# Weight conversion in an attention and softplus kernel: the low words rounded by ScalarE and added by GpSimd, with a new order of the work

## The chip, the core and the metric

The kernel runs on one core of a Trainium2 chip. The metric is the device time of one execution in microseconds; lower is better. The core has five engines with queues of their own: TensorE (PE, whose weight loads are shown apart as PEld), VectorE (DVE), ScalarE (ACT), GpSimd (POOL) and SyncE (SP), which here issues nearly all transfers.

## The reference

Linear attention without softmax, a norm by head, and then two matrix products with softplus between them, for 8 images of 576 rows with 8 heads of 64:

```python
kv  = np.einsum('bhsd,bhse->bhde', k, v)
out = np.einsum('bhsd,bhde->bhse', q, kv)
rms = np.sqrt(np.mean(out * out, axis=-1, keepdims=True) + 1e-06)
x   = (out / rms * g_norm).astype(np.float32)      # then (B,H,S,D) -> (4608, 512)
h = x @ w_in                                        # w_in: 512 x 2048
g = np.maximum(h, 0.0) + np.log1p(np.exp(-np.abs(h)))
return (g @ w_out).astype(np.float32)               # w_out: 2048 x 512
```

The two weight matrices arrive as 64-bit floating-point numbers; everything else is 32 bits wide.

## The kernel before, in words

**Products.** Every matrix product of the feed-forward part is made with operands cut into three pieces: a high one, the remainder, and a third that joins the two. ScalarE makes the high piece, VectorE the others. A product then takes three matrix multiplications.

**Stages.** The feed-forward part works on 16 chunks of 128 inner columns each (c = 0 to 15). In the first stage 12 blocks of 384 tokens go through the first 4 to 6 chunks (`step`: line 864 multiplies x by the first matrix, line 886 is softplus, lines 888, 875 and 879 cut the result into pieces, line 871 multiplies by the second matrix). In the second stage blocks of 512 tokens go through the other chunks, in pairs, by a scheme with fewer products (`wide_step`: lines 1066 and 1137). Partial sums of the first stage are written to memory and read again.

**Attention.** For each image `kv_of` loads keys and values and multiplies them (line 696), and `rows` turns the queries, multiplies (line 720), squares and sums (line 724), takes the root on GpSimd (lines 727 and 728), multiplies by it (line 732) and turns the result for the products (line 738). This is spread over the first 300 us. `split` cuts a tile of x into its pieces (lines 640, 643, 646).

**Weights.** Tile j is chunk c = j // 2 of the first matrix (j even) or of the second (j odd). `weight` fetches one tile of 128x512 doubles (512 KB, line 423) into a raw buffer, of which there is one ("raw") and, for the odd tiles of the first eight chunks, another one ("rawb"). Then it makes 32-bit numbers of it. The high word is moved into the form of a 32-bit number in two VectorE steps (lines 438 and 442). ScalarE squares the top 16 bits (line 434), so that VectorE's mask (line 447) can set numbers that are too small to zero; ScalarE also counts those beyond a limit (line 451). In the version before, three more VectorE steps add the rest of the mantissa: line 455 takes the power of two of the number, line 460 multiplies it by the low word, and line 464 adds the product to the number. After that `split_weight` cuts the result into three pieces (lines 501 to 529), or the tile is written back to memory for the second stage (line 482).

**Order.** The order of all instructions is fixed before the launch. Every piece of work is a task with an engine, an assumed duration, a position, tasks that it waits for and buffers that it takes and gives back. The planner (`Plan.order`) goes through them in assumed time: on each engine it takes, of the tasks that can begin, the one with the smallest position. Transfers can also be tied behind a step of the first product. Each queue then runs its instructions strictly in that order. The positions are computed from the lists P0 to P7: `CONVERT` and `FETCH` place the first eight weight tiles, `TAKEN` those of chunks 6 to 15, P4 the row tiles, P5 the images, P6 the loads of the second stage, P7 the first images' loads. Where the plan sees TensorE idle in the beginning, it puts in multiplications of the identity by itself (line 1232), whose result nobody reads.

The two VectorE steps that make the high word, in their order, and the three that follow the mask stand in the listing.

## Time and profile before

| What | Value |
|---|---|
| median of 3 runs | 858.48 us (857.46, 858.48, 860.58) |
| span of the profiled execution | 856.4 us; its own time is not given beside it |
| TensorE busy | 843.0 us (98%) |
| VectorE busy | 704.1 us (82%) |
| ScalarE busy | 520.6 us (61%) |
| GpSimd busy | 76.6 us (9%) |
| bytes moved | 167.07 MB |

The span runs from the first instruction of the profile to the last; the time of a run is a little longer. The profile gives busy time by engine, by stretch of the span, and by group of instructions (line, engine, operation, output and inputs with their shapes, count; busy us and mean ns of one; idle time of the engine before them and what ended it). A busy TensorE is partly modelled, so a difference of a few tenths of a microsecond in its records means nothing. The granted TensorE clock is 1.00 in all stretches.

### The profile page before, as it was taken

How to read it: one execution, taken by the hardware profiler on the slowest of the kernel's cores; microseconds unless marked ns; L12 is line 12 of the kernel's file. 1: busy time of each engine (PE TensorE's matmuls, PEld its weight loads, DVE VectorE, ACT ScalarE, POOL GpSimd, SP SyncE). 2: the span in 40 equal slices, each digit the busy share in tenths (PEclk: the TensorE clock that was granted, in tenths of full speed). 3: DMA queues.
4: the chain of work that ended last, by engine and by line, in shares of the span. 5: the costliest groups of instructions: out<-in, count | busy, mean ns of one | idle time of the engine just before them, and what ended most of it. 6: DMA issues, size and time to landing. Idle time of an engine off the chain costs nothing.

```text
span 856.4 us, 17075 instructions
## 1 busy us (share of the span) xinstructions
PE 843.0 (98%) x6464; PEld 754.1 (88%) x6464; DVE 704.1 (82%) x995; ACT 520.6 (61%) x980; POOL 76.6 (9%) x79
## 2 busy tenths in 40 slices
PE   8899999999999999999999999999999999999998
PEld 5578898999898999999999999998999899999996
DVE  7888898888788889798898788878788766788873
ACT  6766665446344567766667665655868555566654
POOL 0351223111113300000000000000000000000000
PEclk9999999999999999999999999999999999999999
DMA  9998997778884755436644546645364753777864
GB/s 283 297 233 212 261 273 232 185 245 218 214 188 119 194 160 185 142 110 207 210 156 154 180 151 206 195 158 181 124 197 138 234 168 102 240 237 246 249 189 131
DMA packets 239778, 167.07 MB, mean 195 GB/s; under 512 B 106320, under 2 KB 198736, under 8 KB 239696
## 3 DMA queue, kind: packets, MB, share of 16 engines
q1 hardware_dynamic: 239392, 165.86, 65.9%
q8 instruction: 50, 0.82, 0.4%
q14 instruction: 32, 0.26, 0.1%
q10 hardware_dynamic: 304, 0.13, 0.1%
HBM read 112.98 MB, written 52.95 MB: 194 GB/s over the span
## 4 chain that ended last, share of the span: by engine, by line
PE 94%; ACT 1%; DVE 1%; DMA 1%; issue 1%; POOL 0%; SPq 0%; POOLq 0%; DVEq 0%; ACTq 0%
PE banks L1137 31%; PE banks L1066 28%; PE banks L871 16%; PE banks L864 15%; PE banks L720 2%; PE banks L696 2%; DMA loads<-in_k_dram 1%; PE banks L738 0%; PE banks L1232 0%; PE banks L776 0%; DVE units L643 0%; DVE half L732 0%; DVE roots L724 0%; POOL roots L728 0%; ACT w L783 0%
## 5 line engine op out<-in xcount | busy, mean ns | idle before, releaser
L1137 PE MATMUL banks<-pieces,gv 128*128 128x512 f32 x768 | 236.8, 390 | 0.0
L1137 PE MATMUL banks<-pieces,g_False 128*128 128x512 f32 x384 | 149.4, 389 | 0.0
L1137 PEld LDWEIGHTS banks<-pieces,gv 128*128 128x128 f32 x768 | 132.5, 188 | 17.2 <-DVE banks L910 0.2
L864 PE MATMUL banks<-units,pieces 128*128 128x384 f32 x768 | 144.8, 337 | 0.0
L871 PE MATMUL banks<-pieces,gv 128*128 128x512 f32 x576 | 143.3, 393 | 0.0
L864 PEld LDWEIGHTS banks<-units,pieces 128*128 128x128 f32 x768 | 134.7, 188 | 4.5
L871 PEld LDWEIGHTS banks<-pieces,gv 128*128 128x128 f32 x576 | 106.2, 188 | 19.0
L1066 PEld LDWEIGHTS banks<-units,pieces 128*128 128x128 f32 x840 | 111.0, 188 | 6.5 <-ACT banks L1112 0.4
L1066 PE MATMUL banks<-units,pieces 128*128 128x256 f32 x840 | 115.2, 280 | 0.0
L886 ACT ACTIVATE half<-banks 128x384 f32<-128x384 f32 x64 | 31.4, 491 | 94.0 <-PE banks L864 90.7
L1127 DVE TENSOR_TENSOR gv<-g_True,gv 128x1024 fp32r<-128x1024 f32 x47 | 57.5, 1223 | 35.6 <-ACT gv L1124 35.5
L1137 PEld LDWEIGHTS banks<-pieces,g_False 128*128 128x128 f32 x384 | 72.1, 188 | 15.0
L1066 PEld LDWEIGHTS banks<-units,w 128*128 128x128 f32 x504 | 66.7, 188 | 3.7 <-ACT banks L1112 0.2
L1066 PE MATMUL banks<-units,w 128*128 128x256 f32 x504 | 69.6, 280 | 0.0
L728 POOL TENSOR_TENSOR roots<-roots,half 128x8 f32<-128x8 f32 x36 | 62.3, 1731 | 3.0
L1130 DVE SCALAR_TENSOR_TENSOR g_False<-gv 128x1024 fp32r<-128x1024 f32 x47 | 57.6, 1225 | 1.5
L1029 DVE TENSOR_TENSOR units<-loads,units 128x1024 fp32r<-128x1024 f32 x42 | 51.2, 1219 | 6.0 <-ACT units L1026 5.9
L1094 ACT ACTIVATE g_True<-banks 128x256 f32<-128x256 f32 x96 | 36.7, 384 | 30.6 <-PE banks L1066 29.9
L1116 DVE TENSOR_TENSOR g_True<-banks,g_True 128x512 f32<-128x512 f32 x48 | 33.1, 690 | 25.8 <-PE banks L1066 19.8
L931 ACT ACTIVATE m<-banks 128x512 f32<-128x512 f32 x72 | 42.1, 595 | 18.2 <-PE banks L1137 12.5
L1032 DVE SCALAR_TENSOR_TENSOR units<-units 128x1024 fp32r<-128x1024 f32 x42 | 51.4, 1224 | 1.7
L1026 ACT ACTIVATE units<-loads 128x1024 fp32r<-128x1024 f32 x42 | 44.3, 1056 | 12.4 <-PE banks L1066 10.1
(115 smaller groups left out, 1248.7 us busy)
## 6 DMA issues: line engine op xcount, KB each, us to landing
loads<-x SPq DMA_DIRECT2D x180, 128.0 KB, 2.7
part<-m SPq DMA_DIRECT2D x72, 256.0 KB, 3.1
m<-part SPq DMA_DIRECT2D x72, 256.0 KB, 3.4
loads<-form SPq DMA_DIRECT2D x45, 256.0 KB, 3.2
form<-loads SPq DMA_DIRECT2D x36, 256.0 KB, 3.0
raw<-in_moe_w_in_dram SPq DMA_DIRECT2D x16, 512.0 KB, 4.7
loads<-in_k_dram SPq DMA_DIRECT2D x32, 256.0 KB, 4.0
loads<-in_v_dram SPq DMA_DIRECT2D x32, 256.0 KB, 4.5
```

Of the source, the lines that this page charges most:

```text
L728: nc.gpsimd.tensor_tensor(out=r.tile, in0=r.tile, in1=half, op=ALU.pow)
L864: nc.tensor.matmul(from_the_end(hp, w), lhsT=w_in.tile[:, i, kd * P:(kd + 1) * P], rhs=from_the_end(xv.tile[:, i, kd], w), start=(m == 0), ...
L871: nc.tensor.matmul(mine[i].tile, lhsT=gv.tile[:, m, i * P:(i + 1) * P], rhs=w_out.tile[:, m], start=(c == cs[0] and m == 0), stop=(c == cs ...
L931: a = add("ACT", 690 if ph == LAST else 600, lambda: nc.scalar.activation(new(ot, [P, d_model]), bank.tile, func=AF.Copy, scale=scale if p ...
L1026: nc.scalar.activation(part_of(0, F32R), xl.tile if m > 1 else xl.tile[:, 0], func=AF.Copy, scale=DOWN)
L1029: nc.vector.tensor_tensor(out=part_of(1, F32R), in0=xl.tile if m > 1 else xl.tile[:, 0], in1=part_of(0), op=ALU.subtract)
L1032: nc.vector.scalar_tensor_tensor(out=part_of(2, F32R), in0=part_of(1), scalar=-RADIX, in1=part_of(0), op0=ALU.mult, op1=ALU.add)
L1066: nc.tensor.matmul(from_the_end(place(q), (16, 8)[kd]), lhsT=w[:, m, at:at + P], rhs=from_the_end(dst.tile[:, m, v, kd] if u < 6 else dst. ...
L1094: nc.scalar.activation(dst, src, func=AF.Softplus, scale=1.0 + E)
L1127: nc.vector.tensor_tensor(out=gvt(1, F32R), in0=gt(), in1=gvt(0), op=ALU.subtract)
L1130: nc.vector.scalar_tensor_tensor(out=gt(F32R), in0=gvt(1), scalar=-RADIX, in1=gvt(0), op0=ALU.mult, op1=ALU.add)
L1137: nc.tensor.matmul(from_the_end(mine[i].tile, P), lhsT=(gvt(m, F32R) if m < 2 else gt(F32R))[:, c, i * P:(i + 1) * P], rhs=from_the_end(ou ...
```

## The change

After the mask, the low word is no longer multiplied by the number's power of two and added as a floating-point number. ScalarE reads the low word as an integer, multiplies it by 2^-29 and writes it as a rounded 32-bit integer, which is the number of units in the last place that the low word stands for. GpSimd adds it to the bits of the masked number as integers. The result stays in the buffer of the masked number, so a tile takes two buffers of the ring "m" where it took three, and the raw buffer is given back after the two steps on the high word, the square and the rounding.

The three VectorE steps (lines 455, 460, 464) are gone; the rounding is a new ScalarE task without a wait on VectorE, and the add is a GpSimd task that waits for the mask and the rounding. All lists of positions have new values, and with them the order of every queue may differ.

The diff; of the lists of positions only P0 and P2 are shown:

```diff
--- before.py
+++ after.py
@@ -9,6 +9,7 @@
 F32 = mybir.dt.float32
 F32R = mybir.dt.float32r
 U32 = mybir.dt.uint32
+I32 = mybir.dt.int32
 BF16 = mybir.dt.bfloat16
 AF = mybir.ActivationFunctionType
 ALU = mybir.AluOpType
@@ -252,15 +253,15 @@
     STEPS = [(ph, n, p) for ph in (1, 2) for n in range(n_wide) for p in PAIRS[ph - 1][n]]
     LAST = 2
 
-    P0 = [-45.94, -26.77, -11.8, 0.28, -29.91, -5.64, -2.86, 3.84, -103.4, -98.98, -69.3, -76.66, -68.5, -24.67, -23.22, -34.97, 8.15, -43.02, 7.47, 9.69, 7.18, 18.16, -12.1, 4.75, 1.0, 106.19, 31.3, 6.28, 7.19, 5.22]
...
+    P0 = [-8.08, -21.9, 1.52, -3.72, -1.69, -21.85, -3.44, 4.58, -19.16, -116.42, -126.81, -30.71, -114.11, 66.57, 59.07, -8.96, 11.38, -40.88, 20.33, 9.06, 7.18, 13.51, -12.61, 4.48, 3.76, 2.72, -67.19, 5.29, 10.05, 8.61]
...
     CONVERT, FETCH, EARLY, LATER = P0[:8], P0[8:16], P0[16:27], P0[27:]
...
-    P2 = [24.08, 35.56, 23.68, 37.26, 50.08, 83.13, 74.26, 112.0, 102.25, 108.09, 139.38, -110.13, 88.34, 208.35, 423.47, -209.77, 170.15, -245.78, 423.49, 179.94, -7.53]
...
+    P2 = [28.72, 32.86, 29.3, 39.52, 59.02, 78.06, 93.3, 120.52, 78.04, 106.2, 67.37, 66.51, 64.28, 60.53, 65.65, 67.32, 70.96, 65.85, 87.14, 65.55, -8.62]
...
     SPLIT = {p: (P1[i], P1[6 + i]) for i, p in enumerate((2, 3, 4, 5, 6, 7))}
     TAKEN = {c: (P2[c - 6], P2[4 + c]) for c in range(6, 16)}
     LEAD, APART, AHEAD, MM2, LATE, SPLIT_G = P3[0], P3[1], P3[2], P3[3:11], P3[11:14], P3[14]
@@ -425,7 +426,7 @@
 
         f = add("SP", 450, fetch, (), fetch_pos, [raw], size=1800, behind=behind)
         if wide:
-            sq, t, p = (slot(n) for n in ("sq", "m", "m"))
+            sq, t, r = slot("sq"), w, slot("m")
 
             def words_of():
                 return raw.tile[:, :, 0], raw.tile[:, :, 1]
@@ -451,27 +452,21 @@
                 nc.scalar.activation(sq.tile, sq.tile, func=AF.Identity, scale=2.0 ** -126, bias=big,
                                      accum_out=over[:, j:j + 1])
 
-            def power():
-                nc.vector.tensor_scalar(out=new(p, [P, d_model], U32), in0=t.tile, scalar1=0xFF800000,
-                                        scalar2=None, op0=ALU.bitwise_and)
-
-            def rest():
-                pf = p.tile.bitcast(F32)
-                nc.vector.scalar_tensor_tensor(out=pf, in0=words_of()[0], scalar=2.0 ** -52, in1=pf,
-                                               op0=ALU.mult, op1=ALU.mult)
+            def rounded():
+                nc.scalar.activation(new(r, [P, d_model], I32), words_of()[0], func=AF.Copy, scale=2.0 ** -29)
 
             def total():
-                nc.vector.tensor_tensor(out=new(w, [P, d_model]), in0=t.tile.bitcast(F32),
-                                        in1=p.tile.bitcast(F32), op=ALU.add)
+                nc.gpsimd.tensor_tensor(out=t.tile.bitcast(I32), in0=t.tile.bitcast(I32),
+                                        in1=r.tile, op=ALU.add)
+                t.tile = t.tile.bitcast(F32)
 
             a1 = add("ACT", 670, square, [f], pos, [sq], [raw])
+            a2 = add("ACT", 670, rounded, [f], pos, [r], [raw])
             d1 = add("DVE", 430, high1, [f], pos, [t], [raw])
             d2 = add("DVE", 690, high2, [d1], pos, [], [raw])
             d3 = add("DVE", 690, mask, [d2, a1], pos, [])
             over_done.append(add("ACT", 910, beyond, [d3], pos + (4 if c < 4 else 0), [], [sq]))
-            d4 = add("DVE", 430, power, [d3], pos, [p, w])
-            d5 = add("DVE", 690, rest, [d4], pos, [], [raw])
-            ready = add("DVE", 690, total, [d3, d5], pos, [], [t, p])
+            ready = add("POOL", 1200, total, [d3, a2], pos, [], [r])
         else:
             ready = add("DVE", 450, lambda: nc.vector.tensor_copy(new(w, [P, d_model]), raw.tile[:, :, 0]),
                         [f], pos, [w], [raw])
```

12 lines of the change are left out of this document (6 added, 6 removed).

## The prediction

> **What bounds the kernel now.** I read the profile page first, then TensorE's filler matmuls by stretches, then all engines by stretches, then the groups of the weight conversion, then single instructions of GpSimd and VectorE in order of time. The head of the page:
>
> ```profile
> span 856.4 us, 17075 instructions
> PE 843.0 (98%) x6464; PEld 754.1 (88%) x6464; DVE 704.1 (82%) x995; ACT 520.6 (61%) x980; POOL 76.6 (9%) x79
> PE   8899999999999999999999999999999999999998
> ```
>
> TensorE is busy for 98% of the span, so all that can be won lies in its other 13.4 us and in busy time that is not useful. Useless busy time exists: line 1232 multiplies the identity by itself where the plan saw TensorE idle. Its windows (columns: stretch, length, TensorE busy with these instructions, weight loads, granted clock, DMA share, GB/s):
>
> ```profile
> 0.00:20.00 20.00, 10.99 (x29) 6.92 (x29) 1.00 0.96 286
> 20.00:40.00 20.00, 5.21 (x15) 2.43 (x15) 1.00 1.05 298
> 40.00:60.00 20.00, 2.14 (x7) 1.24 (x7) 1.00 0.94 228
> 60.00:80.00 20.00, 0.50 (x1) 0.19 (x1) 1.00 0.85 214
> 80.00:856.00 776.00, 0.00 (x0) 0.00 (x0) 1.00 0.64 189
> ```
>
> All engines in other stretches (busy us: TensorE, its loads, VectorE, ScalarE, GpSimd; then clock, DMA share, GB/s):
>
> ```profile
> 0.00:4.70 4.70, 3.09 (x7) 2.49 (x8) 1.59 (x7) 1.28 (x1) 0.69 (x6) 1.00 0.54 168
> 4.70:60.00 55.30, 47.40 (x651) 35.74 (x649) 49.15 (x82) 41.72 (x82) 16.94 (x17) 1.00 1.02 280
> 60.00:80.00 20.00, 19.89 (x253) 16.45 (x252) 17.45 (x32) 11.76 (x24) 6.28 (x6) 1.00 0.85 214
> 80.00:140.00 60.00, 60.00 (x585) 53.71 (x585) 54.16 (x93) 37.09 (x73) 15.61 (x14) 1.00 0.90 244
> 140.00:300.00 160.00, 160.00 (x1528) 144.09 (x1528) 135.70 (x235) 76.25 (x151) 37.03 (x36) 1.00 0.76 203
> 300.00:560.00 260.00, 260.00 (x1600) 236.94 (x1599) 223.77 (x298) 172.14 (x327) 0.00 (x0) 1.00 0.54 172
> 560.00:856.00 296.00, 292.63 (x1852) 264.63 (x1850) 222.29 (x253) 180.40 (x324) 0.00 (x0) 1.00 0.59 185
> ```
>
> The reader is to see two kernels in one. From 80 us to the last matmul TensorE never stops and has no fillers: nothing in there can be shortened by relieving VectorE, it can only be lengthened. Before that lies the ramp. Between 4.7 and 60 us TensorE idles 55.30 - 47.40 = 7.9 us, and fillers take 10.99 + 5.21 + 2.14 less the 3.09 before 4.7, that is 15.25 us. These 23.2 us are the ceiling of any gain. In the ramp VectorE is busy 49.15 of 55.30 us (89%) and the DMA share is 1.02. Either of them may set it. VectorE's part in it shows in the order of its work: the first real step of the feed-forward part begins at 44 us, the seventh weight is converted only at 54 us, and the eighth is begun at 60 us:
>
> ```profile
> 44.09 2.07 PE L864 MATMUL banks<-units,pieces 128*128 128x384 f32 x11
> 54.39 0.68 DVE L464 TENSOR_TENSOR m<-m,m 128x512 f32<-128x512 f32 x1
> 60.02 0.42 DVE L438 TENSOR_SCALAR m<-g 128x512 uint32<-128x512 uint32 x1
> ```
>
> **The change, removed.** Of each of the 32 weight tiles three VectorE instructions go (columns of the groups: busy us, mean ns, idle before):
>
> ```profile
> L455 DVE TENSOR_SCALAR m<-m 128x512 uint32<-128x512 uint32 x32 | 13.6, 424 | 1.2 <-DMA part<-m 0.4
> L460 DVE SCALAR_TENSOR_TENSOR m<-raw,m 128x512 f32<-128x512 uint32 x24 | 16.5, 686 | 0.5
> L460 DVE SCALAR_TENSOR_TENSOR m<-g,m 128x512 f32<-128x512 uint32 x8 | 5.5, 692 | 0.2
> L464 DVE TENSOR_TENSOR m<-m,m 128x512 f32<-128x512 f32 x32 | 22.0, 687 | 0.7
> ```
>
> Together 13.6 + 16.5 + 5.5 + 22.0 = 57.6 us, 1.80 us for one weight. Seven weights are converted before 60 us: 7 x 1.80 = 12.6 us of VectorE leave the ramp. The other 25 leave stages in which TensorE is full: worth nothing.
>
> **Added on ScalarE.** One more pass over the raw words for each weight. Its nearest row reads the same buffer over as many elements:
>
> ```profile
> L434 ACT ACTIVATE sq<-raw 128x512 bf16<-128x512 bf16 x24 | 16.1, 673 | 2.7 <-DMA raw<-in_moe_w_in_dram 2.1 <-DMA raw<-in_moe_w_out_dram 0.5
> ```
>
> It costs 0.67 us, 32 x 0.67 = 21.5 us in all, 4.7 us in the ramp, where ScalarE is idle 55.30 - 41.72 = 13.6 us. I take it as hidden; bounds are 0 and 4.7 us, if ScalarE's order puts each one ahead of a copy that TensorE waits for. It can run while VectorE assembles the high word.
>
> **Added on GpSimd.** One integer add of 128x512 with two SBUF inputs for each weight. The trace has no such instruction. Its rows are these:
>
> ```profile
> L728 POOL TENSOR_TENSOR roots<-roots,half 128x8 f32<-128x8 f32 x36 | 62.3, 1731 | 3.0
> L727 POOL TENSOR_SCALAR roots<-roots 128x8 f32<-128x8 f32 x36 | 13.2, 366 | 205.2 <-DVE roots L724 204.1
> masks.py:199 POOL TENSOR_SCALAR_AFFINE_SELECT early<-early 128x128 f32<-128x128 f32 x1 | 0.3, 292 | 0.1
> ```
>
> Below, the add costs at least the 0.29 us of a quarter as many elements; above, the power's 1.73 us. I take four times the 128x128 row, 1.17 us, since that row is the nearest in kind: it streams elements. The Trainium skill, GPSIMD Engine Reference, § 3.1, gives 4497 ns for a two-input add of 2048 elements against VectorE's 2293 and advises against elementwise work there; scaled to 512 elements that is an estimate of about 1.1 us, so the sum would not move by it, and no run here shows it yet.
>
> The add waits for VectorE's mask and for ScalarE's rounding. Queued behind it on GpSimd is the root of the next row tile (lines 727 and 728, together about 2 us), for which VectorE's line 732 waits, and that sends the transposes to TensorE. So a root can come up to 1.17 us later, and an add up to 2 us later behind a root. GpSimd has the room: 16.94 us of 55.30 in the ramp, and 7 x 1.17 = 8.2 more. After the mask a weight took 0.42 + 0.69 + 0.69 = 1.8 us more on VectorE; now it takes 1.17 us when GpSimd is free. I count the latency as unchanged.
>
> **Does the add hold VectorE?** This is the unknown price that matters. The spread of line 727 (ns: least, median, most), and two moments of the trace:
>
> ```profile
> L727 POOL TENSOR_SCALAR roots<-roots x36: 236/241/891, 23.6 to 286.9; 128x8 f32<-128x8 f32 x36
> 56.05 0.74 DVE L508 SCALAR_TENSOR_TENSOR m<-m,g_col,pieces 128x512 f32<-128x512 f32 x1
> 56.22 0.66 POOL L727 TENSOR_SCALAR roots<-roots 128x8 f32<-128x8 f32 x1 [3.70 <-DVE roots L724]
> 36.27 1.66 POOL L728 TENSOR_TENSOR roots<-roots,half 128x8 f32<-128x8 f32 x1
> 37.06 0.69 DVE L460 SCALAR_TENSOR_TENSOR m<-g,m 128x512 f32<-128x512 uint32 x1
> ```
>
> In the first pair a tiny GpSimd instruction that began within a VectorE instruction with two SBUF inputs ended 0.09 us after it (56.88 against 56.79): it was kept out until VectorE had done. In the second pair VectorE ran a two-input instruction in its usual 0.69 us in the middle of GpSimd's power: no hold, but the power reads only eight elements. So the hold of one add lies between 0 (the second pair) and its whole length, 1.17 us, since an add of 512 elements reads all the time. I take the whole length: the first pair is nearest to two engines that both stream. Then a weight frees not 1.80 but 1.80 - 1.17 = 0.63 us of VectorE, and the ramp 7 x 0.63 = 4.4 us; with no hold 12.6.
>
> The Trainium skill, SBUF — State Buffer, § Who interferes with whom, says that a VectorE instruction with two SBUF inputs and a GpSimd instruction that reads SBUF shut each other out for the whole instruction, whichever is first. The first pair agrees (0.66 us instead of the 0.24 us usual there), the second does not show it for a whole instruction (0.69 us within a 1.66 us power). By the rule the ramp frees 4.4 us, by the second pair alone 12.6.
>
> **Moved.** All lists of positions are new, so every queue's order is (SP's, which issues every load, too). The raw buffer comes free earlier, after line 442 and the rounding, not after line 460: about 1.8 us a weight. One buffer of the ring "m" fewer is in use for each weight. In the weights' fetch order chunk 0 of the first matrix comes third through its buffer (positions -126.8, -114.1 and -19.2 for tiles 2, 4, 0), where it was first. Its place was where the third load is now issued:
>
> ```profile
> 18.78 0.54 SPq L423 DMA_DIRECT2D raw<-in_moe_w_in_dram  x1
> ```
>
> 18.8 us, plus 4.7 us to landing and some 7 us for conversion and split, is 30.5 us: earlier than the 44 us at which it is wanted, and also than 39. I cost it at nothing; if the ramp had shrunk by over 13 us it would be late. For the rest of the new order no row gives a price. Its gain is bounded by the same 23.2 us; for its loss, the cover is TensorE's zero idle after 80 us, so any late tile there is paid in full.
>
> **What is late next.** The transfers. Their share is 1.02 up to 60 us, 0.85 in the 20 us after that and 0.90 in the next 60. If the later work is to begin earlier, its loads must too, and there are free 0.15 x 20 = 3.0 us of transfers by 80 us and 3.0 + 0.10 x 60 = 9.0 by 140 us. I take the middle, 6 us, as the most that transfers let the whole move forward without leaving out early loads.
>
> **Sum.** VectorE frees 4.4 us at the least in the ramp, transfers allow 6: I take 5 us. From 80 us on nothing changes. The last 3.4 us without TensorE stay. So the span is 856.4 - 5 = 851.4. The page gives no time of the profiled execution beside its span; the median of the three runs, 858.48, is 2.1 us above the span (1.1 to 4.2 for the single runs), and I leave these 2.1 us as they are: 853.5 us, 0.6% faster. The bounds of this case are 4.4 - 2 (roots behind adds) and 9 us of gain: 849.5 to 856. About 0.5% or 4.3 us is what a measurement of this kernel can tell from no change.
>
> **The rivals.**
> First, the ramp shrinks by more: no hold, 12.6 us less VectorE, and transfers that were early in the old order (third image's keys and values, say) put off. For it: fillers and idle time of 23.2 us leave room. Against: the 1.02. With 10 us it ends at 848.5.
>
> Second, hidden anyway: transfers alone set the ramp. For it: the main queue took 97.4% of 16 engines' time over the first 60 us.
>
> ```profile
> q1 hardware_dynamic: 33629, 16.14, 97.4%
> ```
>
> Against: much of these 16.14 MB is not for the first steps. Then VectorE merely idles more: 858.5 us.
>
> Third, slower: GpSimd's adds hold VectorE where TensorE has no slack. The place is line 875 and line 879, which make the pieces that line 871 multiplies, and their like in the later stage. The nearest slack there is what VectorE waits before line 875:
>
> ```profile
> 86.94 0.56 DVE L875 TENSOR_TENSOR gv<-half,gv 128x384 fp32r<-128x384 f32 x1 [0.49 <-ACT gv L888]
> ```
>
> A hold of 1.17 us less 0.49 is 0.68 us, and 25 adds come after the ramp: 17 us, and 853.5 + 17 = 870. For it: VectorE is busy 54.16 of 60 and 135.70 of 160 us, and mostly with two-input instructions. Against: each conversion also takes 1.80 us out of the same queue, and TensorE runs a step ahead. The point from which it decides is (5 + 4.3) / 25 = 0.37 us lost to TensorE for one add; near it the time is 863. The rule of SBUF — State Buffer in the Trainium skill, named above, speaks for this rival.
>
> **How the numbers follow.** Forecast 0.40, of which 0.06 lies within 0.5%; more gain 0.17; hidden 0.13; slower 0.30, of which 0.01 I count as within. Faster 0.34 + 0.17 = 0.51, same 0.06 + 0.13 + 0.01 = 0.20, slower 0.29. The predicted time is the forecast's. The range reaches below to 846 (12.6 us of gain) and above to 867, which leaves out the worst of the third rival; the forecast's own range is 849.5 to 856.
>
> **What would show it.** Right: fillers in the first 60 us fall by some 5 us, line 864 begins near 39 us, VectorE's total falls by about 57 us and ScalarE's rises by about 21, the new adds on GpSimd take 1.0 to 1.8 us each, and TensorE is full from about 75 us on. Holds show as VectorE instructions of 1 us and more, or gaps before them, at the adds. Wrong: an add far above 1.8 us; TensorE idle or stretched in the 80 to 300 us stretch; fillers as many as before.

## The result: slower, and the profile after

The changed kernel takes 866.56 us (median of 4 runs, 865.24 to 867.65) where the kernel before takes 857.97 us beside it (4 runs, 857.38 to 860.58). The ratio is 1.0091, 95% interval 1.0072 to 1.0111. Measured once more it was 1.0067 (1.0048 to 1.0086). So the change costs 6.3 to 8.6 us; forecast were 5 us of gain.

The head of the page of the changed kernel: span, then busy time of each engine.

```profile
span 864.4 us, 17073 instructions
PE 845.9 (98%) x6456; PEld 755.3 (87%) x6456; DVE 666.6 (77%) x899; ACT 535.4 (62%) x1012; POOL 124.6 (14%) x111
```

VectorE is relieved by 704.1 - 666.6 = 37.5 us, not by the 57.6 us of the removed instructions: 20.1 us have come back inside other VectorE instructions, 0.63 us for each of the 32 adds. (With a bitwise-or on VectorE in the add's place, a run below, nothing comes back: 704.1 - 57.6 + 21.9 = 668.4 us, and 668.8 were measured.) GpSimd has 48 us more. The span has grown by 8.0 us and TensorE's busy time by 2.9 us.

All engines of the changed kernel in three stretches (stretch, length, then busy us of TensorE, its loads, VectorE, ScalarE, GpSimd; granted clock, DMA share, GB/s):

```profile
4.70:60.00 55.30, 43.59 (x537) 33.05 (x536) 36.28 (x58) 41.64 (x83) 25.14 (x22) 0.94 0.95 258
60.00:80.00 20.00, 19.26 (x283) 16.79 (x282) 15.31 (x25) 13.38 (x27) 7.20 (x8) 1.00 0.91 227
140.00:300.00 160.00, 160.00 (x1531) 144.80 (x1532) 125.50 (x204) 82.49 (x163) 50.29 (x46) 1.00 0.73 196
```

In the ramp VectorE is now busy for 36.28 of 55.30 us instead of 49.15, and yet TensorE got through 537 matmuls instead of 651 (of different sizes; what that is worth follows below). The relieved engine idles, and taking work from it did not shorten the ramp. The transfers have slackened too (258 GB/s instead of 280).

The first real step of the feed-forward part in the changed kernel, and the three links of its chain of waits in the first 60 us that are transfers (start, duration, what):

```profile
49.73 4.47 PE L859 MATMUL banks<-units,pieces 128*128 128x384 f32 x24
...
2.26 6.46 DMA loads<-in_k_dram
19.66 5.49 DMA loads<-in_k_dram
38.51 4.68 DMA loads<-in_k_dram
```

That step begins 49.73 - 44.09 = 5.6 us later than before, but with two blocks' matmuls at once (24; the kernel before began its second 12 at 49.30 us). In the kernel before, the chain has two such links in that time:

```profile
4.81 4.79 DMA loads<-in_k_dram
12.59 5.90 DMA loads<-in_k_dram
```

The last keys of image 0 are issued at 19.66 us instead of 12.59 and land at 25.15 instead of 18.49: in the new order five weight tiles stand ahead of them on SyncE's queue, in the old one four. TensorE's wait for keys in the first 60 us is 5.0 us, where it was 0.7 before (and 1.1 for values). Of the 5.0 us, 3.04 lie before the first keys' matmuls, which begin at 8.86 us instead of 8.43; the old order fills most of that time with fillers. For image 0's last keys it is 0.76 us, for keys of image 1 it is 1.18. The first row is of the changed kernel, the second of the kernel before (engine, tile, line, what it waited for: us in all, times, longest):

```profile
PE banks L691 <- DMA loads<-in_k_dram: 5.0, 3, 3.0
```

```profile
PE banks L696 <- DMA loads<-in_k_dram: 0.7, 1, 0.7
```

Just ahead of these keys and the values issued with them SyncE stands still, from 17.55 to 18.68 us, until line 691 on TensorE frees a buffer for loads. The chain of waits goes back from there to ScalarE, where a weight's square, its rounding and one of its pieces follow each other. The first row is SyncE's wait, the others are links of the chain:

```profile
SPq L680 <- PE banks L691: 1.1, 1, 1.1
...
15.32 0.56 ACT sq L435
15.88 0.56 ACT m L456
16.44 0.53 ACT pieces L509
...
18.03 1.08 PE banks L691 x32
```

So keys wait here for a weight's conversion, and one of the new roundings (line 456) is itself a link. No run moved that conversion. Nor is the chain the same each time: in the second measurement of the changed kernel three adds (18.70, 26.67 and 33.11 us) are links where image 0's last keys are one here, and image 1's keys are one in both, and the two executions took 866.55 and 866.49 us. Several chains are about equally long.

Where along the span was the time lost? For this I counted in each stretch the matmuls of the six lines that do useful work, weighed them by the duration of one in the full stages, and compared the running sum with that of before (us of useful work behind; worked out from windows, good to about 1 us, since kernels with the same time as before end between -1.1 and -1.5):

| Kernel | at 60 | at 90 | at 420 | at 450 | at 630 | at 850 |
|---|---|---|---|---|---|---|
| changed | -2.6 | -3.4 | -3.5 | -4.8 | -5.0 | -7.6 |
| changed, second measurement | -2.2 | -3.3 | -3.3 | -4.6 | -4.6 | -7.2 |
| new order, bitwise-or for the add | -1.7 | -2.6 | -3.2 | -3.4 | -3.5 | -5.5 |
| the same, second measurement | -1.2 | -2.2 | -2.9 | -3.2 | -3.3 | -6.7 |
| old order, new operations | 0.0 | 0.2 | -0.5 | -0.6 | -1.2 | -1.5 |

The loss has three places: some 3 us in the ramp, 1.3 us in one go between 420 and 450 us, and 2 to 3 us after 630 us (which is not far above the method's 1 us). Between 90 and 420 us nothing is lost, though 15 of the 32 adds run in that stretch (21.9 us of GpSimd).

The middle one can be seen instruction by instruction. Of the adds' tile: count, then least, median and most duration in ns. Then GpSimd, VectorE and TensorE of the changed kernel in order of time (start, duration, ...; in brackets the idle time before):

```profile
L459 POOL TENSOR_TENSOR m<-m,m x32: 1262/1334/2150, 7.9 to 587.0; 128x512 int32<-128x512 int32 x32
...
427.29 2.15 POOL L459 TENSOR_TENSOR m<-m,m 128x512 int32<-128x512 int32 x1 [4.89 <-issue]
...
427.08 1.22 DVE L1027 SCALAR_TENSOR_TENSOR units<-units 128x1024 fp32r<-128x1024 f32 x1
428.21 2.31 DVE L1122 TENSOR_TENSOR gv<-g_True,gv 128x1024 fp32r<-128x1024 f32 x1
430.45 0.68 DVE L985 TENSOR_TENSOR loads<-loads 128x512 f32<-128x512 f32 x1
431.05 1.21 DVE L1125 SCALAR_TENSOR_TENSOR g_False<-gv 128x1024 fp32r<-128x1024 f32 x1
...
432.32 0.50 PE L1132 MATMUL banks<-pieces,g_False 128*128 128x512 f32 x1 [0.36 <-DVE g_False L1125]
```

The add is issued 0.21 us into line 1027 and takes 2.15 us instead of 1.26, about as much longer as line 1027 still runs (1.01 us). Line 1122 is issued while the add runs and takes 2.31 us instead of its usual 1.22 us: it was held for 1.09 us, until the add had ended at 429.44. Line 1125 is late by that much, and TensorE stops for it, by the trace for 0.36 us, and its weight load for 0.78 us. Each engine held the other once, in the order in which they came. The Trainium skill, SBUF — State Buffer, § Who interferes with whom, says just this of a VectorE instruction with two SBUF inputs and a GpSimd instruction that reads SBUF; here the trace agrees, with 0.89 us in the one direction and 1.09 us in the other.

### The profile page after: what moved, and what is told of

Its sections match the earlier page's. It is cut to its first block, busy times and chain, and to the rows that moved or that the text cites. A ratio compares the mean times of both kernels' runs of the same rounds, so it can differ in the third digit from the quotient of the medians.

```text
span 864.4 us, 17073 instructions
## 1 busy us (share of the span) xinstructions
PE 845.9 (98%) x6456; PEld 755.3 (87%) x6456; DVE 666.6 (77%) x899; ACT 535.4 (62%) x1012; POOL 124.6 (14%) x111
## 4 chain that ended last, share of the span: by engine, by line
PE 93%; DMA 2%; DVE 2%; SPq 1%; ACT 1%; issue 1%; DVEq 0%; ACTq 0%
PE banks L1132 29%; PE banks L1061 27%; PE banks L859 16%; PE banks L866 15%; PE banks L691 2%; PE banks L715 2%; DMA loads<-in_k_dram 2%; PE banks L733 1%; SPq L761 0%; PE banks L771 0%; SPq L680 0%; SPq L613 0%; PE banks L1227 0%; DVE gv L1122 0%; DVE loads L985 0%
## 5 line engine op out<-in xcount | busy, mean ns | idle before, releaser
L1132 PE MATMUL banks<-pieces,gv 128*128 128x512 f32 x696 | 215.3, 391 | 0.2 <-DVE banks L905 0.2
L866 PE MATMUL banks<-pieces,gv 128*128 128x512 f32 x576 | 143.2, 393 | 0.0
L1061 PEld LDWEIGHTS banks<-units,pieces 128*128 128x128 f32 x1014 | 133.0, 188 | 7.7 <-ACT banks L1107 1.4
L1061 PE MATMUL banks<-units,pieces 128*128 128x256 f32 x1014 | 139.3, 281 | 0.0
L859 PEld LDWEIGHTS banks<-units,pieces 128*128 128x128 f32 x768 | 134.8, 188 | 4.6
L1132 PE MATMUL banks<-pieces,g_False 128*128 128x512 f32 x348 | 135.5, 389 | 0.4 <-DVE g_False L1125 0.4
L1132 PEld LDWEIGHTS banks<-pieces,gv 128*128 128x128 f32 x696 | 120.5, 188 | 16.6 <-DVE banks L905 0.6
L866 PEld LDWEIGHTS banks<-pieces,gv 128*128 128x128 f32 x576 | 106.3, 188 | 19.0
L459 POOL TENSOR_TENSOR m<-m,m 128x512 int32<-128x512 int32 x32 | 48.1, 1503 | 325.9 <-DVE m L448 169.4
L1122 DVE TENSOR_TENSOR gv<-g_True,gv 128x1024 fp32r<-128x1024 f32 x47 | 60.7, 1291 | 28.0 <-ACT gv L1119 27.8
L1132 PEld LDWEIGHTS banks<-pieces,g_False 128*128 128x128 f32 x348 | 65.3, 188 | 14.7 <-DVE g_False L1125 0.8
L870 DVE TENSOR_TENSOR gv<-half,gv 128x384 fp32r<-128x384 f32 x64 | 39.3, 614 | 29.8 <-ACT gv L883 23.7
L1107 ACT COPY banks<-banks 128x256 f32<-128x256 f32 x48 | 17.3, 361 | 58.2 <-PE banks L1061 58.0
```

The costliest lines, as they stand in the source:

```text
L459: nc.gpsimd.tensor_tensor(out=t.tile.bitcast(I32), in0=t.tile.bitcast(I32), in1=r.tile, op=ALU.add)
L859: nc.tensor.matmul(from_the_end(hp, w), lhsT=w_in.tile[:, i, kd * P:(kd + 1) * P], rhs=from_the_end(xv.tile[:, i, kd], w), start=(m == 0), ...
L866: nc.tensor.matmul(mine[i].tile, lhsT=gv.tile[:, m, i * P:(i + 1) * P], rhs=w_out.tile[:, m], start=(c == cs[0] and m == 0), stop=(c == cs ...
L870: nc.vector.tensor_tensor(out=gv.tile[:, 1], in0=g.tile, in1=gv.tile.bitcast(F32)[:, 0], op=ALU.subtract)
L1061: nc.tensor.matmul(from_the_end(place(q), (16, 8)[kd]), lhsT=w[:, m, at:at + P], rhs=from_the_end(dst.tile[:, m, v, kd] if u < 6 else dst. ...
L1122: nc.vector.tensor_tensor(out=gvt(1, F32R), in0=gt(), in1=gvt(0), op=ALU.subtract)
```

## The experiments

The theories. **Order:** the loss comes from the new positions, that is, from what each queue is made to do first. **Hold:** it comes from the adds on GpSimd, which shut VectorE out. And the prediction's own premise, **relief:** less VectorE work makes the ramp shorter. Times are medians; "before" was run beside each on the same chip.

| Run | Time, us | Before, us | Ratio (95% interval) |
|---|---|---|---|
| old order, new operations | 860.80 | 858.65 | 1.0023 (1.0012 to 1.0034) |
| old order, bitwise-or | 859.49 | 858.65 | 1.0013 (1.0002 to 1.0024) |
| new order, bitwise-or | 863.73 | 858.65 | 1.0055 (1.0036 to 1.0075) |
| before, idle adds | 863.06 | 858.65 | 1.0057 (1.0041 to 1.0074) |
| before, idle writes | 859.09 | 858.97 | 1.0000 (0.9988 to 1.0012) |
| before, last keys later | 865.09 | 858.97 | 1.0067 (1.0042 to 1.0091) |
| before, last keys earlier | 858.95 | 858.97 | 1.0000 (0.9988 to 1.0013) |
| before, first 13 fillers only | 859.95 | 858.97 | 1.0005 (0.9992 to 1.0017) |
| new order, tile behind the keys | 867.43 | 859.52 | 1.0092 (1.0071 to 1.0112) |
| new order, tile put off | 866.23 | 859.56 | 1.0084 (1.0069 to 1.0099) |
| the same, bitwise-or | 866.25 | 859.56 | 1.0084 (1.0068 to 1.0101) |
| changed kernel again | 865.42 | 859.14 | 1.0067 (1.0048 to 1.0086) |
| new order, bitwise-or, again | 864.43 | 859.14 | 1.0059 (1.0040 to 1.0079) |
| the same with idle adds | 866.55 | 859.14 | 1.0084 (1.0064 to 1.0103) |

### The operations without the order, and the order without the add

The order of before on all queues, with the new operations in the place of the old ones:

```diff
-                nc.vector.tensor_scalar(out=new(p, [P, d_model], U32), in0=t.tile, scalar1=0xFF800000, ...)
+                nc.scalar.activation(new(p, [P, d_model], I32), words_of()[0], func=AF.Copy, scale=2.0 ** -29)
...
-                nc.vector.scalar_tensor_tensor(out=pf, in0=words_of()[0], scalar=2.0 ** -52, in1=pf, ...)
...
-                nc.vector.tensor_tensor(out=new(w, [P, d_model]), in0=t.tile.bitcast(F32), in1=p.tile.bitcast(F32), op=ALU.add)
+                nc.gpsimd.tensor_tensor(out=new(w, [P, d_model]).bitcast(I32), in0=t.tile.bitcast(I32), in1=p.tile, op=ALU.add)
```

> The order of all queues of the kernel before, with the new operations in it: ScalarE's rounding stands where the first of the three removed VectorE steps was planned, GpSimd's add where the last one was. Theory 'order' (the loss comes from the new order of the queues, above all from loads that bring image 0's last keys later): not slower than before, 853 to 858 us, first feed-forward matmul no later than 44.1 us. Theory 'hold' (the adds keep VectorE out, and that is the loss): slower than before, 862 to 867 us. Theory of the prediction (VectorE sets the ramp): 853 to 854 us.

The same order, with the join on VectorE as one bitwise-or; nothing is added on GpSimd, so VectorE is relieved and never held:

```diff
+                nc.scalar.activation(new(p, [P, d_model], I32), words_of()[0], func=AF.Copy, scale=0.937 * 2.0 ** -29)
+                nc.vector.tensor_tensor(out=new(w, [P, d_model]).bitcast(U32), in0=t.tile, in1=p.tile.bitcast(U32), op=ALU.bitwise_or)
```

> The old order again, with ScalarE's rounding (scaled so that it gives 0 to 7), but the low bits put in by one VectorE step (bitwise or) where the last of the three removed steps stood; nothing on GpSimd but the roots. VectorE is relieved of 1.11 us for each weight and nothing can be held. Theory of the prediction (VectorE sets the ramp): 7 x 1.11 = 7.8 us less, 850 to 852 us. If transfers or the static order set the ramp: 857 to 858.5 us. Against the run with GpSimd's add in the same order it shows what the add costs: nothing by 'order', 5 us or more by 'hold'.

And the order of the changed kernel with that bitwise-or:

```diff
-                nc.gpsimd.tensor_tensor(out=t.tile.bitcast(I32), in0=t.tile.bitcast(I32), in1=r.tile, op=ALU.add)
+                nc.vector.tensor_tensor(out=t.tile, in0=t.tile, in1=r.tile.bitcast(U32), op=ALU.bitwise_or)
```

> The new order as it is, with VectorE's bitwise or in the place of GpSimd's add (the rounding scaled to 0 to 7). Theory 'order': 864 to 867 us as with the add. Theory 'hold': 858 to 861 us, VectorE's groups at lines 870 and 1122 back at 555 and 1223 ns.

The old order with the bitwise-or: busy time of each engine, the ramp (windows, columns as above), and its first feed-forward matmuls of the block of 384 tokens:

```profile
PE 843.9 (98%) x6464; PEld 754.7 (88%) x6464; DVE 670.5 (78%) x931; ACT 535.5 (62%) x1012; POOL 74.8 (9%) x79
...
4.70:60.00 55.30, 46.76 (x643) 35.51 (x642) 40.41 (x66) 44.32 (x88) 16.04 (x17) 0.97 1.01 275
...
45.45 2.26 PE L862 MATMUL banks<-units,pieces 128*128 128x384 f32 x12
```

VectorE has 33.6 us less to do, 8.7 us of it in the ramp, with no add to hold it, and the first feed-forward matmul does not begin earlier (45.45 us; 44.09 before; 43.77 with the add on GpSimd). The time is 0.8 us above that of before, not below. So relief is worth nothing in the old order, though it is not quite a pure relief: in the first 60 us VectorE waits 2.0 us for the rounding before the bitwise-or. The theory on which the sum of the prediction rested has fallen. The new operations with the add cost 0.23% there, with the bitwise-or 0.13%. The new order with the bitwise-or costs 0.55%, which is 5.1 us. Of these 0.8 us are those of the operations; the same operations in the two orders are 863.73 - 859.49 = 4.2 us apart. So the larger part of the loss goes with the order.

### What an add does to an engine that otherwise does what it did before

The kernel before, with one add on GpSimd behind each conversion, over buffers that are dead by then; nobody reads what it writes:

```diff
                                         in1=p.tile.bitcast(F32), op=ALU.add)
+                nc.gpsimd.tensor_tensor(out=p.tile.bitcast(I32), in0=t.tile.bitcast(I32),
+                                        in1=p.tile.bitcast(I32), op=ALU.add)
```

> The kernel before, unchanged, with one more 128x512 integer add on GpSimd behind each weight's conversion, of the two buffers that are dead by then; its result is read by nobody. It measures the hold alone: VectorE's other groups should grow by some 20 us in all if each add keeps a two-input instruction out for about 1.08 us as in the changed kernel's trace. Theory 'order': 858 to 860 us, since most of the hold falls where VectorE has room. Theory 'hold': 862 to 867 us.

And with two writes of the same tile in the add's place, which read nothing:

```diff
                                         in1=p.tile.bitcast(F32), op=ALU.add)
+                for _ in range(2):
+                    nc.gpsimd.memset(p.tile.bitcast(F32), 0.0)
```

> The control for the kernel before with an idle add behind each conversion: two GpSimd instructions that only write 128x512 in the add's place, with the same waits and the same place in GpSimd's queue, but no reading. If the loss of the idle adds comes from the reads that shut VectorE's second input out: back to 858 to 859.5 us, VectorE's groups at their old durations. If it comes from roots that wait behind the adds on GpSimd, or from buffers that come free later: 861 to 864 us again.

Groups of the run with adds (busy us, mean ns, idle before), then the group of writes and one VectorE group of the run with writes:

```profile
L467 POOL TENSOR_TENSOR m<-m,m 128x512 int32<-128x512 int32 x32 | 44.8, 1401 | 348.1 <-DVE m L465 307.4 <-ACT g_True L1097 20.2 <-issue 10.1
L882 DVE SCALAR_TENSOR_TENSOR gv<-gv 128x384 fp32r<-128x384 f32 x64 | 39.2, 613 | 6.3 <-DVE gv L878 0.5 <-PE banks L874 0.5
L443 DVE SCALAR_TENSOR_TENSOR m<-g,m 128x512 uint32<-128x512 uint32 x8 | 9.4, 1172 | 0.2
```

```profile
L467 POOL MEMSET m<- 128x512 f32 x64 | 35.0, 547 | 352.0 <-DVE m L464 256.3 <-DMA loads<-x 60.3 <-ACT g_True L1096 20.4
L881 DVE SCALAR_TENSOR_TENSOR gv<-gv 128x384 fp32r<-128x384 f32 x64 | 35.7, 557 | 5.5
```

Before, the two VectorE groups stood at 35.7 us (557 ns) and 5.5 us (690 ns). With 44.8 us of reading adds beside them VectorE is busy 720.5 us in all instead of 704.1, 16.4 us longer, and the kernel 4.4 us slower; with 35.0 us of writes nothing moves. So it is the reading that holds, not that GpSimd is busy or that it writes. The same section of the Trainium skill has it so (an instruction that only writes does not contend); the rows agree.

Of the 16.4 us some 4.4 reach the end, and they are lost early: worked out as in the table above, the profiled execution of this run (864.85 us, the slowest of its four) is 1.6 us behind at 60 us, 5.7 at 90 us and 6.2 at 850 us. After 90 us, where 23 of the adds run, hardly anything is lost. In the old order with the new operations the adds stand in the same ramp, but VectorE is relieved, and there the table has 0.0 at 60 us and 0.2 at 90 us. So VectorE does matter in the ramp, on one side: more time on it costs, less gains nothing.

### One transfer in the old order

The kernel before, with image 0's last keys issued later, behind the fifth weight tile, and in a second run one place earlier, ahead of the fourth; the order written by the planner is otherwise kept (code shortened):

```diff
-    for t in plan.order():
+    planned = plan.order()
+    ...
+    third.start = 20330
+    for t in sorted(planned, key=lambda t: t.start):
         t.run()
```

(14080 in the second run.)

> The kernel before with one transfer moved: the last keys of image 0 are loaded behind the fifth weight tile and five other loads, not before them. Nothing else differs. Theory 'order' (image 0's last keys release the ramp, and the new order brings them later): their landing moves by 4 to 6 us, the first feed-forward matmul from 44.1 to 47 to 50 us, the time to 861 to 864 us. If the ramp has another bound: 858 to 859 us.

> The kernel before with the same transfer one place earlier, ahead of the fourth weight tile. Theory 'order': the keys land 1 to 2 us earlier and the time falls by as much, 856.5 to 857.5 us. If they are not the bound, or if the weight that is now later is one as well: 858 to 860 us.

The run with the keys later, in order of time:

```profile
19.43 0.51 SPq L685 DMA_DIRECT2D loads<-in_k_dram  x1
...
24.02 1.12 PE L696 MATMUL banks<-loads 128*64 128x64 f32 x16 [5.42 <-DMA loads<-in_k_dram]
...
51.00 2.28 PE L864 MATMUL banks<-units,pieces 128*128 128x384 f32 x12
```

One transfer issued 19.43 - 12.59 = 6.8 us later makes TensorE idle for 5.42 us, the first feed-forward step comes 6.9 us later, and the time rises by 6.1 us by the medians (ratio 1.0067), so nearly all of it is kept to the end. Issuing it one place earlier gains nothing (1.0000). So the place of one transfer among SyncE's first is worth about as much as the whole change, and the old order has these keys early enough. This shows that such a move costs so much, not yet that it is what happened in the changed kernel.

### The same transfer in the new order

To see whether the weight tile ahead of the keys makes the new order's loss, the changed kernel with this tile's transfer behind the keys:

```diff
+    chunk0 = [t for t in planned if t.run.__name__ == "fetch" and t.start == 17480][0]
+    chunk0.start = 22000
```

> The changed kernel with one transfer moved: the weight tile that SyncE issues at 17.18 us (524 KB) is issued behind the last keys of images 0 and 1 (19.66 us) instead of ahead of them. Theory (in the new order the ramp is set by image 0's last keys, which land at 25.15 us because weight tiles stand in front of them): 524 KB at some 260 GB/s are 2.0 us, the keys land near 23.2 us, the first feed-forward matmul begins up to 2 us before its 49.73 us, and the time falls from 866.56 to 864.5 to 866 us. If the moved tile (4.8 us later) is itself what the first feed-forward matmul waits for, that matmul comes later than 49.73 and the time rises by up to 2 us. If the order of the matmuls alone sets the ramp, both stay: 866.5 us.

TensorE and ScalarE of this run in order of time:

```profile
23.94 0.69 PE L691 MATMUL banks<-loads 128*64 128x64 f32 x16
...
29.78 0.49 PE L715 MATMUL banks<-early,w 64*64 64x64 f32 x8 [2.26 <-ACT early L699]
...
26.43 0.67 ACT L456 ACTIVATE m<-raw 128x512 int32<-128x512 uint32 x1 [2.71 <-DMA raw<-in_moe_w_in_dram]
...
29.28 0.35 ACT L699 COPY early<-banks 128x256 f32<-128x256 f32 x1
```

The keys are no longer waited for at 25 us, and another wait has taken that place: in ScalarE's written order the moved tile's rounding (line 456) stands ahead of the copy of image 0's key-value products (line 699), so ScalarE now waits 2.71 us for the tile, and TensorE 2.26 us for ScalarE. The first feed-forward step began at 52.04 us. None of the three expectations had that wait.

So the tile's first six steps on ScalarE, VectorE and GpSimd were put behind that copy too, and the same was done with the bitwise-or:

```diff
+    later("fetch", 17480, 22000)
+    later("high1", 23780, 27450)
+    later("high2", 24330, 27460)
+    later("mask", 25920, 28020)
+    later("total", 26730, 28100)
+    later("rounded", 24460, 28000)
+    later("square", 25130, 28010)
+    later("beyond", 27040, 28340)
```

> The changed kernel with the fifth weight tile put off as a whole: its transfer behind the last keys (as in the run before), and its first six steps too, which stood on ScalarE, VectorE and GpSimd ahead of image 0's copy of the key-value products (line 699) and now stand behind it, at most 4 us later in the written order. Theory (loads and written order interlock; with both moved nothing waits in front of image 0): no wait for keys at 25 us, no 2.3 us wait behind the tile's rounding, the first feed-forward matmul begins 1 to 2.5 us before 49.73 us, and the time falls to 864 to 865.8 us. If the loss in the ramp has its cause elsewhere in the new order (image 1's keys, issued at 38.5 us and landing at 43.2, are the next suspect): first matmul near 49.7 us or later, 866 to 867.5 us.

> The same kernel without the integer add on GpSimd: the low word is rounded to 0 to 7 by ScalarE and or-ed into the high word by VectorE (which differs from the reference's words by up to a unit in the last place). By the hold theory it stands 2.5 to 3.5 us below the run beside it, as the new order with the bitwise-or stood 2.8 us below the changed kernel: 861 to 863 us. If the holds matter only where the ramp is tight: the same within 1 us.

Both waits are gone (the keys' matmuls run at 24.96 us without idle time before them), and yet the first feed-forward step begins at 49.72 us, to 0.01 us where it was in the changed kernel; the time is 866.23 us. The rows of this run say why that does not clear the tile (in order of time, by engine):

```profile
26.90 0.67 ACT L456 ACTIVATE m<-raw 128x512 int32<-128x512 uint32 x1 [0.37 <-DMA raw<-in_moe_w_in_dram]
28.96 1.26 POOL L459 TENSOR_TENSOR m<-m,m 128x512 int32<-128x512 int32 x1 [4.12 <-DVE m L448]
30.26 0.72 ACT L496 ACTIVATE pieces<-m,g_down 128x512 fp32r<-128x512 f32 x1 [0.53 <-POOL m L459]
30.89 0.35 ACT L778 COPY w<-banks 128x256 f32<-128x256 f32 x1
...
31.29 1.12 PE L771 MATMUL banks<-ident_r,early 128*128 128x128 f32 x4 [2.23 <-ACT w L778]
```

The tile's cutting into pieces (line 496) was not moved. It waits for the tile's add, and a copy of queries (line 778), which stands behind it on ScalarE, keeps TensorE waiting for 2.23 us; in the changed kernel that wait is 0.30 us, at 28.76 us. Nor did the keys come much earlier: SyncE waits 2.4 us for line 691 ahead of them, issues them at 20.26 us instead of 19.66, and their matmuls start only 0.23 us sooner. So one wait was put in the place of another again, and this run neither shows that the tile is the cause nor rules it out. The next suspects, image 1's keys (38.51 to 43.19 us in the chain of the changed kernel) and the conversion that TensorE's line 691 waits behind, were not moved. Which of the new positions carries the ramp's 3 us stays open.

The bitwise-or gained nothing here (866.25 us), where it had seemed to gain 2.8 us in the new order as it is (866.56 against 863.73, which were not run side by side). That left the price of the add open.

### The price of the add in the new order

Three runs on one chip: the changed kernel, the new order with the bitwise-or, and that one with an add on GpSimd behind each bitwise-or, over a buffer that is dead by then:

```diff
                 nc.vector.tensor_tensor(out=t.tile, in0=t.tile, in1=r.tile.bitcast(U32), op=ALU.bitwise_or)
+                nc.gpsimd.tensor_tensor(out=r.tile, in0=r.tile, in1=r.tile, op=ALU.add)
```

> The changed kernel once more, beside the two runs below on one chip. If the add on GpSimd costs what the first pair showed (866.56 against 863.73), it stands 2.8 us above the same order with a bitwise-or; if the last pair was right (866.23 against 866.25), it stands level with it.

> The new order with the bitwise-or on VectorE in place of the add once more: 863.7 us if the first pair was right, 865.5 to 866.5 us if the last pair was.

> The run above with an integer add on GpSimd behind each bitwise-or, over a buffer that is dead by then and that nobody reads afterwards: it costs nothing but its hold of VectorE (and a buffer that comes free some 1.3 us later). By the hold theory VectorE is busy some 15 to 20 us longer, as it was in the old order (+16.4 us), and the time is 2 to 4.5 us above the run above. If the add's price in the changed kernel is its own latency between the mask and the split and not the hold, the time is the run's above within 1 us.

Measured: 865.42, 864.43 and 866.55 us. The head of the last one and of the run without adds (the second fence):

```profile
PE 846.7 (98%) x6456; PEld 755.2 (87%) x6456; DVE 679.2 (78%) x931; ACT 535.2 (62%) x1012; POOL 116.1 (13%) x111
```

```profile
PE 846.8 (98%) x6456; PEld 756.1 (88%) x6456; DVE 669.1 (78%) x931; ACT 535.8 (62%) x1012; POOL 76.5 (9%) x79
```

Adds that nobody waits for lengthen VectorE's time by 10.1 us (15 to 20 were expected; these adds read one tile twice and take 1.24 us on average) and the kernel by 2.1 us by the medians. That is within the 2 to 4.5 us that the hold theory gave, but the intervals of the two ratios overlap (1.0040 to 1.0079 and 1.0064 to 1.0103). Against the changed kernel the bitwise-or gains 1.0 us. Taken together: the add's price in the new order came out as 2.8, 0.0 and 1.0 us in three pairs, and 1.3 us in the old order. It is of the order of 1 us, and the runs do not fix it closer. The order with the rounding and the bitwise-or costs 5.1 and 5.3 us in its two measurements, of which 0.8 us are the operations' in the old order.

### The late loss

The 2 to 3 us after 630 us stand in the new order with the add and without, and not in the old one. TensorE's weight loads may show a part of it. Their waits from 300 us to the end: the changed kernel, the new order with the bitwise-or (second measurement), and before:

```profile
PEld banks L1061 <- ACT banks L1107: 1.8, 8, 0.2
PEld banks L1061 <- DVE g_True L1111: 0.8, 3, 0.3
PEld banks L1132 <- DVE g_False L1125: 0.8, 1, 0.8
PEld banks L1132 <- DVE banks L905: 0.8, 2, 0.6
PEld banks L1061 <- ACT banks L1103: 0.2, 1, 0.2
```

```profile
PEld banks L1060 <- ACT banks L1106: 1.8, 8, 0.2
PEld banks L1060 <- DVE g_True L1110: 1.3, 5, 0.4
PEld banks L1131 <- DVE banks L904: 0.9, 2, 0.6
PEld banks L1060 <- ACT banks L1102: 0.2, 1, 0.2
```

```profile
PEld banks L1066 <- ACT banks L1112: 0.6, 3, 0.2
PEld banks L1137 <- DVE banks L910: 0.2, 1, 0.2
```

The new order has 4.4 and 4.2 us of such waits where the old one has 0.8; the old order with the new operations has 1.2 and with the bitwise-or 0.8. The one of 0.8 us for line 1125 is the hold at 430 us shown above, and it is there only with the add. The others go with the order. But after 630 us, where the loss is, they are 2.1 us in the changed kernel and 2.7 us with the bitwise-or, against 0.6 before, and TensorE itself hardly stops there (from 630 to 850 us it is busy for 219.99 and 219.90 of 220 us). So they can account for a part of the late loss at most; no run moved them alone, and its cause stays open.

### Fillers and the clock

In the changed kernel the granted clock is 0.94 in the ramp, where it was 1.00. To see what that may cost, the kernel before with only its first 13 filler matmuls; the rest is left out:

```diff
+        if len(warmed) < 13:
             nc.tensor.matmul(new(s, [P, 4, P]), lhsT=ident_r, ...)
+        warmed.append(s)
```

> The kernel before with only the first 13 fillers of line 1232; the other 39 are left out, everything else keeps its order. Theory 'clock' (idle stretches of TensorE in the ramp cost granted clock, as the 0.71 at 10 to 15 us of the changed kernel shows): the granted clock falls below 1.00 in stretches of the ramp and the time rises by 1 to 4 us, 860 to 862 us. If fillers do nothing: 857 to 858.5 us.

The granted clock fell to 0.89 in the first 20 us and 0.94 in the next 20, was 1.00 after that, and the time rose by 0.05% (-0.08% to 0.17%). So a lower clock in the ramp costs nothing that can be measured here. In the changed kernel it fell later, to 0.50 from 44 to 46 us, where TensorE is on the chain of waits: the turning of a result (line 733) took 1.12 us there instead of 0.66. But in the second measurement of that kernel the profiled execution had 1.00 in all of the first 60 us, began the first feed-forward step at 49.27 us instead of 49.73, and took 866.55 us, the other 866.49. So the clock is not the loss either.

## Why the prediction was wrong, step by step

- **"Two kernels in one", and the ceiling.** That nothing can be won after 80 us, only lost, was right, and it was half of the answer: of the changed kernel's 7.6 us some 4 were lost there. The 23.2 us of idle time and fillers are a ceiling that no run has come near: the best ones are level with before.
- **"Either of them may set it", then VectorE taken.** This is the step that failed first. The quoted rows (89% busy, the eighth weight begun at 60 us) say that VectorE was busy, not that TensorE waited for it. The chain of waits before the first feed-forward matmul had transfers of keys in it, and I did not follow it. With 8.7 us less VectorE work in the ramp and no hold, the first feed-forward matmul began no earlier (45.45 us against 44.09). The 4.4 to 12.6 us of this term measured 0: time on VectorE in the ramp has a price when it grows (the idle adds), none when it shrinks. The signs fell as well: of the first 60 us fillers take 16.2 us where they took 18.3, 2.2 us less instead of 5, and line 864's step began not near 39 but at 49.73 us.
- **"For the rest of the new order no row gives a price."** The gain was bounded by 23.2 us and the loss left at "paid in full", and neither went into the sum. It is the largest term: 4.2 us between the two orders with the same operations and no add. A row in the profile of before could have warned of it: the link 12.59 to 18.49 us of the chain, image 0's last keys. In the old order 6.8 us later cost 6.1 us. That this is what the changed kernel pays is not shown: its keys come 7.1 us later, and its ramp loses some 3 us.
- **"I cost it at nothing": chunk 0's tile third in its buffer.** Whether that was right stays open. Put off still further, the time was as it was (866.23 against 866.56 us), but the tile then stood in the chain of waits itself. What it does to transfers and copies behind it was not in the step.
- **The hold.** The mechanism was right, and so was the size of one: taken 1.17 us, 1.09 us for the one at 430 us. Over all adds VectorE lost 20.1 us, 0.63 us for one, less than one whole hold for each add; some adds wait themselves, like the one of 2.15 us. The second pair of rows (a VectorE instruction at its usual 0.69 us in the middle of the power of eight elements) was no sign against it for instructions that stream. Setting it off against the relief in the ramp was right in kind as well: adds without relief lost some 5.7 us by 90 us, adds with relief nothing. What failed is that something would be left over.
- **The price of the add.** Taken 1.17 us; 1.26 least, 1.33 median, 2.15 most: the most lies above the 1.73 us given as the upper bound, in a case where the add has to wait for a VectorE instruction. The estimate of 1.1 us from GPSIMD Engine Reference, § 3.1, of the Trainium skill was low by a sixth of the median.
- **ScalarE's rounding, hidden.** Nearly right in the old order: about 0.67 us each, and with 32 of them and all else that was new the time stood 0.13 to 0.23% above before. ScalarE's total rose by 14.8 us, not by 21; back-to-back ScalarE instructions overlap in the trace (one from 24.04 to 24.69 us, the next from 24.59), which may be the difference. In the new order one rounding is a link of the chain of waits (15.88 us), and in the run with the tile moved one stood ahead of a copy that TensorE waited for: the very case that the step named as its upper bound.
- **The rivals.** The third had the right side, and its 863 to 870 us hold the result, as does the stated range, which reached to 867 for its sake; but that is luck, for its place was wrong: it put 25 losses of 0.68 us at lines 875 and 879, in the stretch where TensorE is full. From 90 to 420 us, with 15 adds in it, the running sum lost 0.1 us, so holds there are absorbed. One hold, at 430 us, got through, and the running sum falls by 1.3 us there. "Hidden anyway" (858.5) is what the relief alone came to: 859.49.

## What to carry to other kernels

An engine that is busy for 89% of a stage need not be what the stage waits for: before a relief is priced, follow the chain of waits to the stage's first useful instruction, and see whether that engine is in it. Where a change renews the whole order of the queues, price the order first: find the transfers on the chain, and read which loads, and which waits of the queue that issues them, the new order puts in front of them. Here one transfer's 6.8 us later issue cost 6.1 us, and an earlier one won nothing. Work moved from VectorE to GpSimd that reads SBUF isn't taken off VectorE: of the 57.6 us taken away 20.1 came back. And a run that moves a task without all that hangs on it shows a new wait, not the price of the old one: read its chain before drawing the conclusion.

## What the runs showed of the hardware

- An integer add of 128x512 on GpSimd with two SBUF inputs takes 1.26 us at the least and up to 2.15 us when it begins within a VectorE instruction with two SBUF inputs. It held such an instruction that came while it ran for up to 1.13 us (line 870 at 209.88 us of the changed kernel, 1.69 us instead of 0.56). A VectorE instruction with one input was held once, too: in the run with idle adds line 439 took 1.52 us at 425.70 us, instead of 0.42. A write of 128x512 takes 0.55 us, and 64 of them left VectorE's busy time at 704.3 us, where it was 704.1.
- In a queue with a fixed order a removed wait turned into another one: with the weight tile moved behind the keys, TensorE's wait for the keys went and a wait of 2.26 us for ScalarE came; with more of the tile's steps moved that went, and one of 2.23 us came.
- A granted clock of 0.89 and 0.94 in the first 40 us, with three quarters of the fillers left out, did not change the time by an amount that ten runs could tell (0.05%, -0.08% to 0.17%).
